# One explicit activation table set at the head of a fused attention and feed-forward kernel

## The chip, the cores and the metric

The kernel runs on one core of one Trainium2 chip. The metric is the device time of one execution in microseconds (us); lower is better. One core has a matrix engine (PE, with its weight loads listed apart as PEld), a vector engine (DVE), a scalar engine that evaluates functions from a loaded table (ACT), a general engine (POOL, which here issues the input DMAs) and SP, which here issues the output DMAs. Each engine works through its own list of instructions in order and waits for the others at semaphores.

## The reference

Eight batches of eight heads attend over 576 tokens plus 16 "beacon" keys that every query may see; the rest is causal. The attention output of all heads, 512 wide, goes through a feed-forward layer with a leaky ReLU.

```python
B, H, S, Nb, D = (8, 8, 576, 16, 64)
k_all = concatenate([beacon_k, k], axis=2)          # 592 keys
scores = scale * matmul(q, k_all.transpose(0, 1, 3, 2))
scores = where(causal, -1e9, scores)
a = exp(scores - scores.max(-1))
a /= a.sum(-1) + 1e-09
attn = matmul(a, v_all)                             # B,H,S,D -> x of 4608 x 512
h = x @ w_in                                        # 512 -> 2048
return maximum(0.01 * h, h) @ w_out                 # 2048 -> 512
```

## The kernel before

**Tiling.** All matmul operands are bf16. The keys of a head lie in five blocks of up to 128 rows, the queries along the free dimension. For one head `stage_scores` makes six score matmuls (L195, 512, 64, 464, 336, 208 and 80 columns, since blocks on the diagonal skip the queries ahead of them) into PSUM tiles `acc`, and ACT turns each into `aT` with an Exp (L202). DVE multiplies the diagonal blocks with a 0/1 mask (L209, L217). No maximum is subtracted. `stage_av` then multiplies `aT` with `v_aug`, whose rows hold 64 values and 64 ones, so that rows 64 to 127 of `av_ps` hold the sum of each query's weights 64 times over (L233, eight matmuls in two halves of 288 queries: 3 and 5). The division is done on ACT as exp(-ln(sum)): a Ln (L243) from PSUM to `lnd`, an Exp with scale -1 (L246) to `recip`; DVE multiplies and writes the head's part of `xT` (L249).

**The feed-forward part.** `moe1_fchunk` makes 128 of the 2048 hidden features for the 576 tokens of a batch: four matmuls of 512 columns and four of 64 (L260), then a Prelu on ACT for each of the two PSUM tiles (L271: `gT` for 512 tokens, `gtail` for 64). `moe2_tchunk` makes 128 tokens of output from 16 matmuls (L282), a copy by DVE (L290) and an output DMA (L291). The 64-token tails of two batches share one further group of 16 matmuls (L296, `moe2_tailpair`).

**Order.** The program is written as 64 steps, one per head. In a step stand: weight loads and loads for the next batch (POOL), the transposes of a pair of heads in even steps (L168 and L174, PE, with DVE copies at L181 and L182), the scores of the head before, the weighted sum of the head before that, and a share of the feed-forward part of the batch before: four chunks of `moe1_fchunk` in steps 1 to 4 of a batch, one `moe2_tchunk` in steps 5, 6, 7 and step 0 of the next. Batch 0 has no feed-forward work, and after the last head the whole feed-forward part of batch 7 stands alone. A tile framework schedules the instructions of each engine from this and sets the waits. The PSUM pools that tie PE to the others are `ps_acc` (4 buffers, shared by scores and both feed-forward layers; released by ACT's Exp or Prelu, or by DVE's copy) and `ps_av` (2 buffers, one per half head; released when L249 has read them). The input tiles `q_nat`, `k_nat` and `v_aug` have two buffers; before each load of `v_aug` DVE writes its ones with a MEMSET (L147).

**Table loads.** No line of the kernel names a table set. The compiler puts an ACT_TABLE_LOAD on ACT's list where the next function needs one, and the profile writes it down under the line of that function: L243 for Ln, L246 for the Exp of the reciprocal, L202 for the Exp of the scores. Prelu (L271) stands behind an Exp and gets none.

Of the kernel before, what the change touches and what calls it, by code (L numbers as in the profile page):

```python
# [15 lines left out]
def kernel(  # L16
# [11 lines left out]
    nc = tc.nc  # L28
# [29 lines left out]
    OTCH = [(i * 128, min(128, S - i * 128)) for i in range((S + 127) // 128)]  # L58

    QCH = [(0, 288), (288, 288)]  # L60

    singles = ctx.enter_context(tc.tile_pool(name="singles", bufs=1))
    inpool = ctx.enter_context(tc.tile_pool(name="inpool", bufs=2))
# [161 lines left out]
    def stage_av(bt, ht, xT, h):  # L225
        v_aug, aT = bt["v_aug"], ht["aT"]
        for (qs, qw) in QCH:
            av = ps_av.tile([128, 512], FP32, name="av_ps", tag="av_ps")
# [213 lines left out]
```

## Time and profile before

| what | value |
|---|---|
| median of 3 runs | 616.53 us (613.58 to 1085.5) |
| span of the profiled execution | 610.7 us |
| PE / ACT / DVE / POOL busy | 470.3 / 512.6 / 174.1 / 120.4 us |
| ACT_TABLE_LOAD on ACT | 161, at 1283 ns each |
| mean granted clock of PE | 0.905 of full |

The page lists no total time of the profiled execution itself; its span, from the first instruction to the last, is 5.8 us under the median and 2.9 us under the lowest run, and these few microseconds lie around it. Busy times are sums of when an engine had something in it, and a busy PE may be one at half its clock, so the durations of single groups of matmuls say more than its share. "Idle before, <- releaser" names the work that ended an engine's wait. Where several instructions of one line stand together, the profile writes the first one's shape and the count.

### The profile page before, as it was taken

What the parts mean: (1) busy time and instruction counts of PE and PEld (TensorE: products, weight loads), DVE (VectorE), ACT (ScalarE), POOL (GpSimd) and SP (SyncE); (2) the same over time, 40 slices, a digit from 0 to 9 for tenths busy, and PEclk for the clock granted to TensorE, in tenths of its full rate; (3) what the DMA queues carried; (4) which work ended last, traced back from release to release, by engine and by line L of the source; (5) the groups of instructions that cost most, each with busy time, mean ns of one, the idle gap of its engine ahead of it and who ended that gap; (6) DMA issues with size and microseconds to landing.
All of it is one profiled execution on the core that took longest, in us unless ns stands there. A gap on an engine that the chain in (4) does not pass through costs nothing.

```text
span 610.7 us, 7832 instructions
## 1 busy us (share of the span) xinstructions
PE 470.3 (77%) x2766; PEld 226.2 (37%) x2816; DVE 174.1 (29%) x557; ACT 512.6 (84%) x1057; POOL 120.4 (20%) x159
## 2 busy tenths in 40 slices
PE   2867677876798697886888777886858876885696
PEld 1323333433344343443444333443424433442342
DVE  4233321342124412234223521234122421132101
ACT  0899989998999969999999979999799978997640
POOL 9885323020230303103230302303000000000000
PEclk9999888996889988997989978899789988897799
DMA  9999638024660706606561526616000100000002
GB/s 93 152 176 170 41 25 55 35 48 27 40 41 34 75 18 41 57 35 58 38 42 36 64 29 39 41 53 57 1 1 18 52 4 15 0 35 18 19 18 69
DMA packets 123432, 28.57 MB, mean 47 GB/s; under 512 B 115712, under 2 KB 117760, under 8 KB 123392
## 3 DMA queue, kind: packets, MB, share of 16 engines
q0 software_dynamic: 118144, 18.62, 41.3%
q1 hardware_dynamic: 5248, 9.44, 4.5%
q8 instruction: 22, 0.36, 0.3%
q14 instruction: 18, 0.15, 0.1%
HBM read 37.22 MB, written 9.44 MB: 76 GB/s over the span
## 4 chain that ended last, share of the span: by engine, by line
ACT 51%; PE 24%; issue 16%; DVE 6%; POOL 1%; DMA 1%; DVEq 0%; POOLq 0%
ACT L243 14%; PE acc L260 11%; ACT aT L202 11%; ACT L246 9%; ACT recip L246 6%; ACT lnd L243 6%; PE acc L195 5%; ACT gT L271 4%; PE acc L282 4%; DVE osb L290 3%; DVE xT L249 3%; PE acc L296 2%; PE av_ps L233 1%; ACT gtail L271 1%; DMA k_nat<-in_k_dram 1%
## 5 line engine op out<-in xcount | busy, mean ns | idle before, releaser
L260 PE MATMUL acc<-xT,w_in_sb 128*128 128x512 bf16 (+1 forms) x996 | 169.9, 329 | 33.0 <-ACT gT L271 25.2
L202 ACT ACTIVATE aT<-acc 128x512 bf16<-128x512 f32 (+5 forms) x384 | 123.6, 408 | 38.7 <-PE acc L195 37.5
L233 PE MATMUL av_ps<-aT,v_aug 128*128 128x288 bf16 (+4 forms) x512 | 85.3, 273 | 59.1 <-DVE xT L249 59.1
L260 PEld LDWEIGHTS <-w_in_sb 128*128 128x128 bf16 x1024 | 82.7, 111 | 118.9 <-issue 77.8
L249 DVE TENSOR_TENSOR xT<-av_ps,recip 64x288 bf16<-64x288 f32 x128 | 53.5, 447 | 253.9 <-ACT recip L246 253.8
L282 PE MATMUL acc<-w_out_sb,gT 128*128 128x512 bf16 x491 | 114.4, 382 | 0.8
L195 PE MATMUL acc<-qT_sb,kT_sb 64*128 64x512 bf16 (+5 forms) x384 | 82.6, 310 | 30.1 <-ACT gT L271 13.9
L243 ACT ACT_TABLE_LOAD x80 | 102.6, 1283 | 1.4
L246 ACT ACT_TABLE_LOAD x79 | 101.4, 1283 | 1.4
L271 ACT ACTIVATE gT<-acc 128x512 bf16<-128x512 f32 x128 | 76.6, 599 | 28.9 <-PE acc L260 26.6
L233 PEld LDWEIGHTS <-v_aug 128*128 128x128 bf16 (+1 forms) x512 | 41.0, 101 | 107.4 <-issue 80.6
L282 PEld LDWEIGHTS <-gT 128*128 128x128 bf16 x512 | 48.8, 98 | 54.7 <-issue 1.6
L124 POOL DMA_DIRECT2D q_nat<-in_q_dram x40 | 33.9, 878 | 98.1 <-PE tp_ps L168 95.1
L246 ACT ACTIVATE recip<-lnd 64x288 f32<-64x288 f32 x128 | 51.4, 436 | 0.9
L217 DVE TENSOR_TENSOR aT<-aT,mask_reg 128x128 bf16<-128x128 bf16 (+1 forms) x256 | 45.9, 212 | 18.8 <-ACT aT L202 16.4
L195 PEld LDWEIGHTS <-kT_sb 64*128 64x128 bf16 (+1 forms) x384 | 28.7, 102 | 59.8 <-issue 48.6
L243 ACT ACTIVATE lnd<-av_ps 64x288 f32<-64x288 f32 x128 | 46.9, 403 | 4.2 <-PE av_ps L233 3.3
L209 DVE TENSOR_TENSOR aT<-aT,mask_reg 128x112 bf16<-128x112 bf16 x64 | 13.5, 211 | 81.3 <-ACT aT L202 80.3
L148 POOL DMA_DIRECT2D v_aug<-in_beacon_v_dram x8 | 4.4, 548 | 156.2 <-PE av_ps L233 156.0
L140 POOL DMA_DIRECT2D k_nat<-in_k_dram x40 | 33.6, 861 | 1.4 <-DMA w_in_sb<-in_moe_w_in_dram 0.7
L157 POOL DMA_DIRECT2D v_aug<-in_v_dram x40 | 33.7, 868 | 0.0
L290 DVE COPY osb<-acc 128x512 f32<-128x512 f32 x32 | 21.9, 684 | 33.4 <-PE acc L282 33.0
(23 smaller groups left out, 185.0 us busy)
## 6 DMA issues: line engine op xcount, KB each, us to landing
out_dram<-osb SPq DMA_DIRECT2D x32, 256.0 KB, 2.0
q_nat<-in_q_dram POOLq DMA_DIRECT2D x32, 128.0 KB, 4.1
k_nat<-in_k_dram POOLq DMA_DIRECT2D x24, 128.0 KB, 4.1
v_aug<-in_v_dram POOLq DMA_DIRECT2D x24, 128.0 KB, 4.2
w_in_sb<-in_moe_w_in_dram POOLq DMA_DIRECT2D x8, 256.0 KB, 7.0
w_out_sb<-in_moe_w_out_dram POOLq DMA_DIRECT2D x8, 256.0 KB, 9.0
out_dram<-osb SPq DMA_DIRECT2D x8, 128.0 KB, 2.3
k_nat<-in_k_dram POOLq DMA_DIRECT2D x8, 112.0 KB, 3.2
```

Of the source, the lines that this page charges most:

```text
L124: nc.gpsimd.dma_start(out=q_nat[0:rows, ci, :, :], in_=q[b, :, s0 : s0 + rows, :].rearrange("h p d -> p h d"),)
L195: nc.tensor.matmul(out=acc[0:rows, 0:cw], lhsT=kT_sb[p0 : p0 + 64, l0_ : l0_ + rows], rhs=qT_sb[p0 : p0 + 64, c0 : c0 + cw], start=True, s ...
L202: nc.scalar.activation(out=aT[0:rows, ci, c0 - off : c0 - off + cw], in_=acc[0:rows, 0:cw], func=AF.Exp, scale=0.125,)
L217: nc.vector.tensor_tensor(out=aT[0:rows, ci, 0:rows], in0=aT[0:rows, ci, 0:rows], in1=mask_reg[0:rows, 0:rows], op=ALU.mult,)
L233: nc.tensor.matmul(out=av[0:128, lo - qs : qw], lhsT=v_aug[0:rows, ci, h, :], rhs=aT[0:rows, ci, lo - off : qs + qw - off], start=(bi == 0 ...
L243: nc.scalar.activation(out=lnd[0:64, 0:qw], in_=av[64:128, 0:qw], func=AF.Ln)
L246: nc.scalar.activation(out=recip[0:64, 0:qw], in_=lnd[0:64, 0:qw], func=AF.Exp, scale=-1.0)
L249: nc.vector.tensor_tensor(out=xT[(h % 2) * 64 : (h % 2) * 64 + 64, h // 2, qs : qs + qw], in0=av[0:D, 0:qw], in1=recip[0:64, 0:qw], op=ALU ...
L260: nc.tensor.matmul(out=acc[:, 0:tw], lhsT=w_in_sb[:, j, fc * 128 : (fc + 1) * 128], rhs=xT[:, j, ts : ts + tw], start=(j == 0), stop=(j == ...
L271: nc.scalar.activation(out=dst, in_=acc[:, 0:tw], func=AF.Prelu, alpha=0.01,)
L282: nc.tensor.matmul(out=acc[0:tw, :], lhsT=gT[:, fc, t0 : t0 + tw], rhs=w_out_sb[:, fc, :], start=(fc == 0), stop=(fc == NF - 1),)
L290: nc.vector.tensor_copy(out=osb[0:tw, :], in_=acc[0:tw, :])
```

## The change

One call is added ahead of the tile pools. It puts one ACT_TABLE_LOAD of the set `natural_log_exp_and_others`, which holds Exp, Ln and Prelu, at the head of ACT's list. No other line is changed; all later lines move down by two, so that L202 is L204, L243 is L245, and so on.

```diff
     QCH = [(0, 288), (288, 288)]
+
+    nc.scalar.preload_act_table_set("natural_log_exp_and_others")

     singles = ctx.enter_context(tc.tile_pool(name="singles", bufs=1))
```

In the built program ACT has 161 ACT_TABLE_LOADs before and 1 after. The same 896 ACTIVATEs are there. The first place is ACT in batch 0, one step before, where `aT<-acc` are the Exps of the scores, `lnd` the Lns and `recip` the Exps of the reciprocal:

```order
L243 ACT_TABLE_LOAD
L243 ACTIVATE lnd<-av_ps 64x288 x2
L246 ACT_TABLE_LOAD
L246 ACTIVATE recip<-lnd 64x288 x2
L202 ACTIVATE aT<-acc 128x512
L202 ACTIVATE aT<-acc 128x64
L202 ACTIVATE aT<-acc 128x464
```

And the same step with the change:

```order
L245 ACTIVATE lnd<-av_ps 64x288 x2
L248 ACTIVATE recip<-lnd 64x288 x2
L204 ACTIVATE aT<-acc 128x512
L204 ACTIVATE aT<-acc 128x64
L204 ACTIVATE aT<-acc 128x464
```

The two loads are gone and the ACTIVATEs stand as they stood. The second place is ACT where the first feed-forward chunks of a batch stand among the Lns, before:

```order
L246 ACT_TABLE_LOAD
L246 ACTIVATE recip<-lnd 64x288 x2
L271 ACTIVATE gT<-acc 128x512
L271 ACTIVATE gtail<-acc 128x64
L271 ACTIVATE gT<-acc 128x512
L271 ACTIVATE gtail<-acc 128x64
L243 ACT_TABLE_LOAD
L243 ACTIVATE lnd<-av_ps 64x288
L246 ACT_TABLE_LOAD
L246 ACTIVATE recip<-lnd 64x288
```

And with the change:

```order
L245 ACTIVATE lnd<-av_ps 64x288
L248 ACTIVATE recip<-lnd 64x288
L273 ACTIVATE gT<-acc 128x512
L273 ACTIVATE gtail<-acc 128x64
L273 ACTIVATE gT<-acc 128x512
L273 ACTIVATE gtail<-acc 128x64
L245 ACTIVATE lnd<-av_ps 64x288
L248 ACTIVATE recip<-lnd 64x288
```

Here too only the loads have gone. The tile framework orders a few matmuls of the first heads of batch 0 otherwise (114 of PE's 5634 rows move). The third place is PE right after the transposes of the queries of the third pair of heads, before:

```order
L168 MATMUL tp_ps<-ident,q_nat 128x64
L174 LDWEIGHTS k_nat
L174 MATMUL tp_ps<-ident,k_nat 128x128
L174 LDWEIGHTS k_nat
L174 MATMUL tp_ps<-ident,k_nat 128x128
```

And with the change:

```order
L170 MATMUL tp_ps<-ident,q_nat 128x64
L197 LDWEIGHTS kT_sb
L197 MATMUL acc<-qT_sb,kT_sb 128x208
L197 LDWEIGHTS kT_sb
L197 MATMUL acc<-qT_sb,kT_sb 80x80
L176 LDWEIGHTS k_nat
```

The last two scores of the first head now stand ahead of the transposes of the third pair's keys instead of behind them. After the first seven heads PE's list is the same; POOL's and SP's are the same throughout, and on DVE one of two multiplications of the first head (L249) moves by one place.

## The prediction

> **What bounds the kernel now.** I read the page's busy times first, then the groups of instructions for the loads, the waits, and then the time line of single steps, since the share of busy time mixes stages.
>
> ```profile
> PE 470.3 (77%) x2766; PEld 226.2 (37%) x2816; DVE 174.1 (29%) x557; ACT 512.6 (84%) x1057; POOL 120.4 (20%) x159
> ACT 51%; PE 24%; issue 16%; DVE 6%; POOL 1%; DMA 1%; DVEq 0%; POOLq 0%
> L243 ACT ACT_TABLE_LOAD x80 | 102.6, 1283 | 1.4
> L246 ACT ACT_TABLE_LOAD x79 | 101.4, 1283 | 1.4
> DVE xT L249 <- ACT recip L246: 253.8, 79, 4.4
> PE av_ps L233 <- DVE xT L249: 59.1, 48, 2.7
> PE acc L260 <- ACT gT L271: 25.2, 16, 2.5
> ```
>
> ACT is the busiest and carries half of the chain that ended last. Two groups of 159 loads (161 are in the program) take 204.0 us of its 512.6. PE's longest waits are for what lies behind loads: the normalised `xT` that frees `av_ps`, and the Prelu that frees `acc`. One step of batch 0 on ACT shows the loads without cover:
>
> ```profile
> 44.11 1.84 ACT L202 ACTIVATE aT<-acc 128x512 bf16<-128x512 f32 x6
> 45.97 1.28 ACT L243 ACT_TABLE_LOAD   x1
> 47.26 0.70 ACT L243 ACTIVATE lnd<-av_ps 64x288 f32<-64x288 f32 x2
> 47.99 1.28 ACT L246 ACT_TABLE_LOAD   x1
> 49.28 0.78 ACT L246 ACTIVATE recip<-lnd 64x288 f32<-64x288 f32 x2
> 50.08 1.84 ACT L202 ACTIVATE aT<-acc 128x512 bf16<-128x512 f32 x6
> ```
>
> The step is 50.08 - 44.11 = 5.97 us, ACT never rests, and 2.6 us are loads. Each load begins 0.02 to 0.03 us after the ACTIVATE before it and the next ACTIVATE follows at once, so a load costs 1.28 us and little else. The Trainium skill (ScalarE: Activation LUTs, What ACT_TABLE_LOAD costs) adds a drain of about 1.38 us to each switch, 2.66 us in all; by it the 159 would be 423 us. These rows have no room for that drain, so they decide.
>
> It would be wrong to take 204 us off the span: that holds only where ACT sets the pace afterwards too. So I cut the span into five pieces and ask in each what PE needs.
>
> ```profile
> 0.00:22.09 22.09, 11.00 (x51) 4.31 (x51) 7.94 (x15) 5.36 (x14) 20.55 (x32) 1.00 1.46 107
> 22.09:63.88 41.79, 28.71 (x137) 12.80 (x137) 14.83 (x58) 41.21 (x85) 26.85 (x36) 1.00 1.65 160
> 63.88:102.81 38.93, 28.09 (x165) 13.58 (x168) 10.05 (x31) 35.77 (x73) 12.98 (x17) 0.82 0.57 37
> 102.81:530.46 427.65, 340.53 (x2071) 166.41 (x2110) 127.01 (x415) 383.70 (x794) 59.99 (x75) 0.90 0.35 37
> 530.46:610.70 80.24, 61.99 (x346) 29.10 (x352) 14.27 (x40) 46.57 (x97) 0.00 (x0) 0.91 0.09 30
> ```
>
> The columns are the length, then busy us (and instructions) of PE, PEld, DVE, ACT, POOL, then PE's clock, DMA share and GB/s. The pieces are the start to the first Ln, seven heads of batch 0, the first part of batch 1, six whole batches (71.3 us each), and the end.
>
> **Start, 22.1 us: unchanged.** The first load lies under the wait for the inputs (ACT is busy 5.36 of 22.09 us), and so will the new one. The reordered rows of PE lie at the end of this piece: half a dozen transposes of about 0.1 us, either way, taken as 0.
>
> **Seven heads of batch 0, 41.8 to 25.9 us.** Without the loads ACT needs 1.84 + 0.70 + 0.78 and the gaps, 3.35 us per head; that is the lower end. PE is busy 28.71 / 7 = 4.1 us per head here, against 2.15 for the same work further on (below), so it runs at about half speed although the clock column says 1.00. If it stays so slow, PE is the bound at 4.1; but then it works without gaps, and the dense stretches of the later trace ran at full clock. I take the middle, 3.7, and 7 x 3.7 = 25.9; the ends give 23.5 and 28.7. The loads of POOL stay ahead:
>
> ```profile
> 34.94 1.72 POOL L98 DMA_DIRECT2D w_in_sb<-in_moe_w_in_dram  x3
> DMA to landing us min/median/max: 5.5/7.0/8.2
> ```
>
> The last part of `w_in_sb` is issued by 36.66 and lands within 8.2, before 45; the first layer would need it at 22.1 + 25.9 + 1.7 = 49.7.
>
> **A whole batch, 71.3 to 51.5 us (53.3 with the tail group).** PE's price of each part is read where it ran without waits at full clock:
>
> ```profile
> 316.85 0.41 PE L195 MATMUL acc<-qT_sb,kT_sb 64*128 64x512 bf16 x2
> 318.91 3.62 PE L282 MATMUL acc<-w_out_sb,gT 128*128 128x512 bf16 x15
> 363.81 4.08 PE L260 MATMUL acc<-xT,w_in_sb 128*128 128x512 bf16 x31
> 370.06 2.12 PE L260 MATMUL acc<-xT,w_in_sb 128*128 128x512 bf16 x15
> ```
>
> (A matmul or two are missing from some rows; each group has 16 or 32.) The second layer is 4 x 3.6 = 14.4. The first layer has 128 matmuls, 3 x 2.12, 2 x 4.13 (one matmul added to 4.08) and a part of 1.95 at the join of two batches (12 and 4 matmuls beside others), 16.6. Between 316.85 and 318.91 stand a head's six scores, seven of eight weighted-sum matmuls and four transposes, 2.06; with the rest 2.15, and eight heads are 17.2. That is 48.2 us of work. ACT has, per batch, 8 x 3.35 and 16 pairs of Prelus at 0.6 (`gT` at 352.97, the next at 353.57, below), 36.4 us, so it is no longer the bound; PE is.
>
> ```profile
> 352.97 0.60 ACT L271 ACTIVATE gT<-acc 128x512 bf16<-128x512 f32 x1
> 353.57 0.60 ACT L271 ACTIVATE gT<-acc 128x512 bf16<-128x512 f32 x1
> 344.59 0.42 PE L233 MATMUL av_ps<-aT,v_aug 128*128 128x288 bf16 x3
> 345.61 2.19 DVE L147 MEMSET v_aug<- 128x2560 bf16 x1 [1.10 <-PE av_ps L233]
> 347.72 0.40 DVE L217 TENSOR_TENSOR aT<-aT,mask_reg 128x128 bf16<-128x128 bf16 x3
> 349.17 0.81 DVE L249 TENSOR_TENSOR xT<-av_ps,recip 64x288 bf16<-64x288 f32 x2 [1.05 <-ACT recip L246]
> 349.77 0.38 PE L233 MATMUL av_ps<-aT,v_aug 128*128 128x288 bf16 x3 [2.56 <-DVE xT L249]
> 375.05 3.78 PE L260 MATMUL acc<-xT,w_in_sb 128*128 128x512 bf16 x16
> ```
>
> What is left of the waits I walked through for one batch by hand. After a second-layer chunk ACT has 3.62 us for 6 Exps' rest, two Lns and two reciprocals, about 2 us: no wait is left there. At the join of two batches one is, and it changes its cause: DVE's MEMSET of 2.19 us stands ahead of the masks and of `xT`. It starts 0.6 us after the last weighted sum of the old batch (345.01) and holds DVE for 2.5 us with the masks (to 348.12); the first half of `xT` needs about 0.45 more and some start-up, so it ends 3.7 us after that sum. PE has 12 first-layer matmuls (1.6 us) and ten transposes (about 0.75) for that time, 2.35 us, and waits about 1.35 (2.56 before). The Lns and Prelus behind it cost PE, by my estimate from the walk, 0.8 us for the buffers of the next two chunks, the scores behind those 0.85, and smaller waits 0.3: 3.3 us per batch. Sum 48.2 + 3.3 = 51.5. Every second batch has the tail group, 3.6 more; six batches are 6 x 51.5 + 3 x 3.6 = 319.8 (427.65 before).
>
> **First part of batch 1, 38.9 to 27.8 us.** It holds 112 first-layer matmuls, 14.5 us, about three and a half heads, 7.3, and the join, 3.0: 24.8. PE comes into it at half clock, and I add 3.0: the first 16 matmuls took 3.78 instead of 2.12 us after such a wait before (375.05, the row above), and some heads' work stands beside them.
>
> The rows for the end, and for the clock further down:
>
> ```profile
> 571.42 1.12 PE L260 MATMUL acc<-xT,w_in_sb 128*128 128x512 bf16 x4 [4.37 <-DVE xT L249]
> 588.22 13.98 PE L282 MATMUL acc<-w_out_sb,gT 128*128 128x512 bf16 x63
> 602.03 3.62 PE L296 MATMUL acc<-w_out_sb,gtail 128*128 128x512 bf16 x15
> 348.00:350.00 2.00, 0.23 (x3) 0.24 (x4) 0.93 (x4) 1.97 (x4) 2.00 (x3) 1.00 1.60 102
> 352.00:354.00 2.00, 0.38 (x1) 0.10 (x1) 0.45 (x1) 1.96 (x5) 0.00 (x0) 0.50 0.37 23
> ```
>
> **The end, 80.2 to 65.4 us.** By the same prices: 2.1 of the first layer, 4 chunks of 3.6, four rests of heads 2.1 + 1.8 + 1.8 + 2.2 and 0.6 for the last sums, 128 matmuls of the first layer 17.0, a wait of 0.7 for the last `xT` (4.37 before, with four loads in its chain), 64 of the second 14.0, the tail 3.6, and from its end to the end of the span 5.05 as before (602.03 + 3.62 to 610.7).
>
> **The sum.** 22.1 + 25.9 + 27.8 + 319.8 + 65.4 = 461.0 us of span. With the 5.8 us by which the median of the runs, 616.53, is above the profiled span of 610.7, that is 467 us.
>
> **Rivals.** *The clock falls at each join.* Around a wait of 2.56 us PE's clock was halved: 1.00 at 348 to 350, 0.50 at 352 to 354, and 16 matmuls took 3.78 us at 375. I leave about 2 us of waits within some 5 us at the join. Before, the six batches ran at a mean clock of 0.90, which is 42.8 us lost, 7.1 per batch, at two places; if the join keeps its half, 3.5 us in each of seven batches, that is 24.5 us: 491. The Trainium skill (TensorE: Matmul & The Clock Gate, Why this matters for your kernels) wants no idle gap over about 3 us for the clock to stay; by it this rival would not happen and the sum stays 467, but the rows show the clock lost after a gap of 2.56 us, so the chance is not nil: 0.15.
>
> *PE runs through.* If the join's waits are covered (the scheduler's other work fills them), batch 0 goes at ACT's 3.35 and batch 1 begins at full clock, 7 x 3.3 + 2.4 + 3.0 = 28.5 us fall away: 438. Against it: DVE's MEMSET stays where it is. 0.12.
>
> ```profile
> PE acc L195 <- DVE osb L290: 9.6, 26, 0.8
> L202 ACT ACTIVATE aT<-acc 128x512 bf16<-128x512 f32 x64 | 38.5, 602 | 24.9 <-PE acc L195 24.1
> L271 ACT ACTIVATE gT<-acc 128x512 bf16<-128x512 f32 x128 | 76.6, 599 | 28.9 <-PE acc L260 26.6 <-remote 1.5
> ```
>
> *More small waits than I count.* Every step leaves PE, ACT and DVE in a ring through 4 and 2 PSUM buffers; if each of 56 heads loses a further 0.7 us (PE lost up to 0.8 to the output copy before, first row), 39 us: 506. 0.10.
>
> *Slower functions, the other side.* If each ACTIVATE were slower from the combined set, ACT would be the bound again: it has 36.4 us per batch against PE's 51.5, so from 1.4 times the duration on it decides, and at 71.3 / 36.4 = 1.96 times nothing would be won; above 2 times it is slower than 616. At 2.1 times, a batch is 76.4 us, 5 us above before, and the time about 660. Against it: a 128x512 Exp and a 128x512 Prelu, different functions, take 602 and 599 ns. 0.02, half of it slower.
>
> That the loads come back elsewhere can be excluded: the built program holds one.
>
> **How the numbers follow.** The forecast has 0.61, and its own range is 452 to 482 (seven heads of batch 0 from 23.5 to 28.7, waits per batch from 1.5 to 5). With the clock rival inside and half of the other two, the range is 445 to 500. A measurement of this kernel tells about 2% from no change. All cases but slower functions are over 2% faster, 0.98; within 2% 0.01, slower 0.01.
>
> **What would show it.** One ACT_TABLE_LOAD; ACT busy near 306 us; heads of batch 0 every 3.4 to 4.0 us; second-layer chunks every 5.4 us within a batch; batches every 51.5 and 55.1 us; PE the first in the chain with over 60%, its clock at 0.95 or more after batch 1; a wait of PE on `xT` of about 1.4 us left at each join, behind the MEMSET. I am wrong if Exps, Lns or Prelus become longer, if PE's clock still falls in each batch, or if PE waits for ACT in the second-layer steps.

## The result and the profile after

| | kernel before | kernel after |
|---|---|---|
| median, us | 616.19 (4 runs, 613.58 to 1085.5) | 454.88 (4 runs, 454.70 to 455.02) |
| ratio | | 0.739, 95% interval 0.7355 to 0.7434 |
| span of the profiled execution, us | 610.7 | 453.0 |
| mean granted clock of PE | 0.905 | 0.998 |

The forecast was 467 us, 445 to 500. One run of the kernel before took 1085.5 us; the ratio leaves it out. The table loads fell from 161 to one, 160 x 1.283 = 205 us of ACT's work, and the time by 161 us, so 0.79 us per us of load. The measured time lies inside the forecast's range, 12 us under its middle.

From the page of the kernel after: the busy times, PE's clock in 40 slices, and the engines in the chain that ended last.

```profile
PE 421.1 (93%) x2816; PEld 207.4 (46%) x2816; DVE 179.3 (40%) x557; ACT 299.5 (66%) x897; POOL 120.4 (27%) x159
...
PEclk9999999999999999999999999999999999999999
...
PE 72%; ACT 14%; DVE 5%; issue 3%; DMA 3%; POOL 2%; POOLq 0%
```

ACT was first in the chain with 51% and has 14% now; PE carries 72% and is busy 93% of a span in which the clock column no longer falls (for batch 0 the column is wrong, as shown below). The waits of the kernel after (what waited, for what, us in total, times, the longest):

```profile
ACT aT L204 <- PE acc L197: 86.2, 36, 13.5
...
PE av_ps L235 <- DVE xT L251: 7.9, 6, 1.5
...
PE acc L262 <- ACT gT L273: 2.9, 7, 0.6
```

The direction has turned round: ACT now waits 86 us for scores, and PE, which waited 59.1 us for `xT` and 25.2 for Prelus, waits 7.9 and 2.9. The span cut at the same places of the program as in the forecast (length, then busy us of PE, PEld, DVE, ACT, POOL, clock, DMA share, GB/s):

```profile
0.00:21.62 21.62, 10.66 (x50) 4.16 (x51) 7.94 (x15) 5.37 (x13) 20.38 (x32) 1.00 1.45 104
21.62:49.91 28.29, 27.82 (x137) 12.85 (x136) 14.54 (x58) 23.63 (x70) 20.89 (x29) 1.00 1.67 176
49.91:75.10 25.19, 22.61 (x170) 11.78 (x169) 10.05 (x31) 20.26 (x60) 16.62 (x22) 1.00 1.66 122
75.10:388.60 313.50, 302.30 (x2115) 151.07 (x2111) 132.09 (x415) 222.36 (x672) 62.48 (x78) 1.00 0.49 51
388.60:453.00 64.40, 57.71 (x356) 27.58 (x352) 14.66 (x40) 27.87 (x82) 0.00 (x0) 0.99 0.11 38
```

| piece | forecast | measured | difference |
|---|---|---|---|
| start | 22.1 | 21.6 | -0.5 |
| seven heads of batch 0 | 25.9 | 28.3 | +2.4 |
| first part of batch 1 | 27.8 | 25.2 | -2.6 |
| six batches | 319.8 | 313.5 | -6.3 |
| end | 65.4 | 64.4 | -1.0 |
| around the span | 5.8 | 1.9 | -3.9 |

The last row is 454.88 - 453.0. The differences sum to -11.9, from 466.8 before rounding to 454.9.

ACT in two steps beside the second layer (time line of the kernel after: start, length, what; in brackets the rest ahead of it and what ended it):

```profile
239.22 1.85 ACT L204 ACTIVATE aT<-acc 128x512 bf16<-128x512 f32 x6 [2.19 <-PE acc L197]
241.10 0.70 ACT L245 ACTIVATE lnd<-av_ps 64x288 f32<-64x288 f32 x2
241.70 0.77 ACT L248 ACTIVATE recip<-lnd 64x288 f32<-64x288 f32 x2
244.53 1.85 ACT L204 ACTIVATE aT<-acc 128x512 bf16<-128x512 f32 x6 [2.06 <-PE acc L197]
```

A step is 244.53 - 239.22 = 5.31 us and ACT rests about 2.1 of them, always for a score of PE. The Lns follow the Exps without a load. PE in the same steps has no wait at all (the two groups left out have none either):

```profile
240.55 3.62 PE L284 MATMUL acc<-w_out_sb,gT 128*128 128x512 bf16 x16
244.10 0.61 PE L197 MATMUL acc<-qT_sb,kT_sb 64*128 64x512 bf16 x3
244.65 0.64 PE L235 MATMUL av_ps<-aT,v_aug 128*128 128x288 bf16 x5
...
245.85 3.62 PE L284 MATMUL acc<-w_out_sb,gT 128*128 128x512 bf16 x16
```

Most of what is left of PE's waits stands at the joins of two batches. DVE at one join:

```profile
257.93 2.19 DVE L149 MEMSET v_aug<- 128x2560 bf16 x1 [0.67 <-PE av_ps L235]
260.04 0.40 DVE L219 TENSOR_TENSOR aT<-aT,mask_reg 128x128 bf16<-128x128 bf16 x3
260.46 0.82 DVE L251 TENSOR_TENSOR xT<-av_ps,recip 64x288 bf16<-64x288 f32 x2
```

And PE at the same join:

```profile
261.06 0.38 PE L235 MATMUL av_ps<-aT,v_aug 128*128 128x288 bf16 x3 [1.54 <-DVE xT L251]
...
263.04 2.12 PE L262 MATMUL acc<-xT,w_in_sb 128*128 128x512 bf16 x16 [0.39 <-ACT gT L273]
```

The reciprocals were done at 258.31 + 0.77 = 259.08 (not shown), so `xT` waits there for DVE, which is in its MEMSET and the masks until 260.44; PE loses 1.54 us, and 0.39 more behind a Prelu.

### The profile page after: what moved, and what is told of

It reads as the page before. It is cut to its first block, busy times and chain, and to the rows that moved or that the text cites. A ratio compares the mean times of both kernels' runs of the same rounds, so it can differ in the third digit from the quotient of the medians.

```text
span 453.0 us, 7721 instructions
## 1 busy us (share of the span) xinstructions
PE 421.1 (93%) x2816; PEld 207.4 (46%) x2816; DVE 179.3 (40%) x557; ACT 299.5 (66%) x897; POOL 120.4 (27%) x159
## 4 chain that ended last, share of the span: by engine, by line
PE 72%; ACT 14%; DVE 5%; issue 3%; DMA 3%; POOL 2%; POOLq 0%
PE acc L284 24%; PE acc L262 16%; PE acc L197 13%; PE av_ps L235 12%; ACT gT L273 4%; ACT recip L248 3%; PE acc L298 3%; ACT lnd L245 3%; ACT aT L204 2%; DVE v_aug L149 2%; DMA q_nat<-in_q_dram 2%; PE tp_ps L176 2%; DVE xT L251 2%; PE tp_ps L170 2%; ACT gtail L273 1%
## 5 line engine op out<-in xcount | busy, mean ns | idle before, releaser
L204 ACT ACTIVATE aT<-acc 128x512 bf16<-128x512 f32 (+5 forms) x384 | 120.0, 411 | 86.6 <-PE acc L197 86.2
L262 PE MATMUL acc<-xT,w_in_sb 128*128 128x512 bf16 (+1 forms) x1024 | 134.8, 287 | 3.4 <-ACT gT L273 2.9
L262 PEld LDWEIGHTS <-w_in_sb 128*128 128x128 bf16 x1024 | 70.3, 98 | 65.4 <-issue 5.5
L235 PE MATMUL av_ps<-aT,v_aug 128*128 128x288 bf16 (+4 forms) x512 | 81.0, 270 | 9.5 <-DVE xT L251 7.9
L197 PE MATMUL acc<-qT_sb,kT_sb 64*128 64x512 bf16 (+5 forms) x384 | 79.7, 302 | 3.0 <-ACT aT L204 0.7
L284 PEld LDWEIGHTS <-gT 128*128 128x128 bf16 x512 | 48.5, 98 | 53.8
L245 ACT ACTIVATE lnd<-av_ps 64x288 f32<-64x288 f32 x128 | 47.7, 403 | 24.6 <-PE av_ps L235 22.9
L235 PEld LDWEIGHTS <-v_aug 128*128 128x128 bf16 (+1 forms) x512 | 37.8, 102 | 44.3 <-issue 29.8
L219 DVE TENSOR_TENSOR aT<-aT,mask_reg 128x128 bf16<-128x128 bf16 (+1 forms) x256 | 46.4, 212 | 20.6 <-ACT aT L204 15.7
L292 DVE COPY osb<-acc 128x512 f32<-128x512 f32 x32 | 22.1, 691 | 64.8 <-PE acc L284 64.8
L197 PEld LDWEIGHTS <-kT_sb 64*128 64x128 bf16 (+1 forms) x384 | 26.7, 101 | 40.7 <-issue 27.3
L170 PE MATMUL tp_ps<-ident,q_nat 128*128 128x128 bf16 (+1 forms) x160 | 21.6, 231 | 8.7 <-DMA q_nat<-in_q_dram 8.5
L273 ACT ACTIVATE gtail<-acc 128x64 bf16<-128x64 f32 x128 | 28.6, 223 | 0.0
```

The source lines that it names most:

```text
L197: nc.tensor.matmul(out=acc[0:rows, 0:cw], lhsT=kT_sb[p0 : p0 + 64, l0_ : l0_ + rows], rhs=qT_sb[p0 : p0 + 64, c0 : c0 + cw], start=True, s ...
L204: nc.scalar.activation(out=aT[0:rows, ci, c0 - off : c0 - off + cw], in_=acc[0:rows, 0:cw], func=AF.Exp, scale=0.125,)
L219: nc.vector.tensor_tensor(out=aT[0:rows, ci, 0:rows], in0=aT[0:rows, ci, 0:rows], in1=mask_reg[0:rows, 0:rows], op=ALU.mult,)
L235: nc.tensor.matmul(out=av[0:128, lo - qs : qw], lhsT=v_aug[0:rows, ci, h, :], rhs=aT[0:rows, ci, lo - off : qs + qw - off], start=(bi == 0 ...
L245: nc.scalar.activation(out=lnd[0:64, 0:qw], in_=av[64:128, 0:qw], func=AF.Ln)
L262: nc.tensor.matmul(out=acc[:, 0:tw], lhsT=w_in_sb[:, j, fc * 128 : (fc + 1) * 128], rhs=xT[:, j, ts : ts + tw], start=(j == 0), stop=(j == ...
```

## The experiments

All kernels but one (it says so) are the kernel after with one edit, or with two that were tried apart. In the runs that follow the kernel before took 610.97 to 612.61 us on the same chips, and single runs of it spread over 1 to 2%, those of the changed kernels over up to 0.8%; so I compare the changed kernels by their own times with 454.88, and take a difference for real where the trace shows its place. That this can be done across the chips is seen in `half_loads`: up to its edit it keeps within 0.2 us of the kernel after (the last second-layer chunk ahead of it starts at 200.73 and 200.94).

**delay_m2: is ACT off the path beside the second layer?** In the 28 heads of batches 1 to 7 that stand beside a second-layer chunk, the Ln of the first half is repeated three times more: 84 instructions of about 0.4 us, 33 us of ACT that nothing needs.

```diff
-            nc.scalar.activation(
-                out=lnd[0:64, 0:qw], in_=av[64:128, 0:qw], func=AF.Ln
-            )
+            for _ in range(4 if extra and qs == 0 else 1):
+                nc.scalar.activation(
+                    out=lnd[0:64, 0:qw], in_=av[64:128, 0:qw], func=AF.Ln
+                )
...
+                     extra=b >= 1 and h in (0, 5, 6, 7))
```

> 28 heads (those that stand beside a second-layer chunk, batches 1 to 7) repeat the Ln of their first half three times more, about 1.2 us of ACT each, 33 us in all, behind the same waits and with the same result. In the profile of the change ACT rests 2.06 us in each of these steps. Theory (PE sets the pace, ACT has slack there): 455 us, 452 to 460. Rival (ACT still sets the pace, every microsecond on it counts): 455 + 33 = 488.

Measured 456.8 us (456.5 to 457.35). ACT in the same two steps:

```profile
241.26 1.85 ACT L204 ACTIVATE aT<-acc 128x512 bf16<-128x512 f32 x6 [0.87 <-PE acc L197]
...
246.56 1.85 ACT L204 ACTIVATE aT<-acc 128x512 bf16<-128x512 f32 x6 [0.74 <-PE acc L197]
```

The step is still 5.30 us and only the rest shrinks, from 2.1 to 0.8. 33 us of ACT cost 1.9, and that not beside the second layer: the first second-layer chunk starts 2.2 us later than in the kernel after (81.35 against 79.15) and the last group at the end 2.0 (432.52 against 430.49), so the loss lies at the entry into batch 1, where one of the 28 places stands and PE's clock is 0.50 from 58 to 60 in place of 1.00. ACT's work beside the second layer, which the forecast costs at nothing, is covered by PE.

**delay_m2b: where does the cover end?** The same with 7 in the place of 4, 66 us in all, 2.4 per step.

> The same 28 heads repeat that Ln six times more, about 2.35 us of ACT each, 66 us in all, nearly what the two loads per head took. Theory: that is 0.3 us over the slack of 2.06, so each step goes from 5.3 to 5.6 or a little more, 463 to 472 us. Rival (all of it counts): 521. Rival (ACT's time does not matter at all): 455.

Measured 472.19 us (471.35 to 472.58), 17.3 more than without. ACT has no rest left:

```profile
243.33 1.86 ACT L204 ACTIVATE aT<-acc 128x512 bf16<-128x512 f32 x6
245.21 3.20 ACT L246 ACTIVATE lnd<-av_ps 64x288 f32<-64x288 f32 x8
248.45 0.78 ACT L249 ACTIVATE recip<-lnd 64x288 f32<-64x288 f32 x2
249.25 1.84 ACT L204 ACTIVATE aT<-acc 128x512 bf16<-128x512 f32 x6
```

This step is 249.25 - 243.33 = 5.92 us, 0.62 above 5.30. That 28 x 0.62 = 17.4 comes near the 17.3 is chance. A whole batch is 1.8 to 2.0 us longer, some 0.46 for each of its four steps, and 4.0 us are lost ahead of the first of them (83.19 against 79.15), behind a wait at the entry into batch 1:

```profile
56.59 0.59 PE L235 MATMUL av_ps<-aT,v_aug 128*128 128x288 bf16 x3 [3.33 <-DVE xT L252]
```

The forecast had 0.3 us a step or a little more and no loss at the entry; the result is 0.2 us above its range. Beside the second layer ACT becomes the bound once about 2 us are added to a step. The two loads that stood in each such step were 2 x 1.28 = 2.57 us, beyond that cover.

**half_loads: do the loads explain the whole difference?** One Sqrt of 64 x 8 elements behind the first Ln of batch 4, whose result nothing reads. Sqrt is not in the preloaded set, so from there on the compiler again places a load at each turn between Ln and Exp.

```diff
+            if extra and qs == 0:
+                junk = singles.tile([64, 8], FP32, name="junk")
+                nc.scalar.activation(
+                    out=junk[0:64, 0:8], in_=lnd[0:64, 0:8], func=AF.Sqrt
+                )
...
+                     extra=s - 2 == 4 * H)
```

> The changed kernel with one small extra ACTIVATE (a square root of 64x8 into a tile that nobody reads) behind the first Ln of batch 4. It forces another table, and from there on the compiler places real loads as in the kernel before; up to there the program has the one load. Theory (the gain is made step by step wherever loads are gone): 210 us as in the changed kernel up to that place, then 325 as before, 2 around the span: 537, 525 to 550, with PE's clock at 0.99 in the first part and 0.90 in the second. Rival (the gain comes from the start, from the order of batch 0 or from a clock that stays up once it is up): 455 to 470.

Measured 541.13 us (539.62 to 544.12). The page's two groups of loads (busy us and mean ns), then the span cut where they begin (columns as above):

```profile
L253 ACT ACT_TABLE_LOAD x41 | 52.6, 1283 | 0.7
L245 ACT ACT_TABLE_LOAD x41 | 52.6, 1283 | 0.7
```

```profile
0.00:210.00 210.00, 189.20 (x1219) 93.02 (x1240) 91.81 (x283) 141.55 (x423) 91.82 (x124) 1.00 1.02 87
210.00:538.30 328.30, 257.51 (x1548) 125.29 (x1577) 84.51 (x275) 270.30 (x559) 28.52 (x36) 0.90 0.27 32
```

With two single ones more, 84 loads came back, 107.8 us, and cost 541.13 - 454.88 = 86.3: 0.80 us per us. The 76 that stay away, 97.5 us, then account for the other 75.0 of the gain, 0.77 per us. PE's clock is 1.00 before the place and 0.90 behind it, inside one execution. So the gain follows the loads in both parts alike, and the lost clock of the kernel before followed from them. A load takes 1.28 us and the next ACTIVATE starts 0.01 us behind it (one that begins at 332.35 is followed by a Ln at 333.64). The Trainium skill (ScalarE: Activation LUTs, What ACT_TABLE_LOAD costs) has a drain of about 1.38 us beside it at each switch; no row here shows one.

The rate of 0.8 is a mean over unlike parts: the six batches gained 114.2 us for 120 loads, 0.74 per us, and the first part of batch 1 gained 13.7 for 12, 0.89. Inside a batch it differs more. One batch of the kernel before, cut at PE's second-layer chunks: three steps beside the second layer, then the rest (one more such step, the join and the first layer).

```profile
318.91:338.81 19.90, 17.10 (x97) 8.23 (x97) 7.82 (x27) 18.39 (x39) 0.00 (x0) 1.00 0.10 35
338.81:390.51 51.70, 40.73 (x262) 20.12 (x265) 14.09 (x43) 45.53 (x97) 13.64 (x17) 0.87 0.59 48
```

And the same batch of the kernel after:

```profile
235.25:251.86 16.61, 16.61 (x99) 7.79 (x97) 8.26 (x26) 9.73 (x32) 0.00 (x0) 1.00 0.33 61
251.86:289.52 37.66, 35.47 (x267) 18.13 (x265) 14.52 (x44) 27.39 (x83) 13.64 (x17) 1.00 0.72 57
```

The three steps lost six loads, 7.7 us, and gained 3.3, 0.43 per us, since PE's own 5.30 us stand close behind ACT's. The rest lost 14 loads, 18.0 us, and gained 14.0, 0.78 per us, and only there had the clock fallen. So most of the gain was made where `delay_m2` and the next two runs change nothing; what bounds the steps beside the first layer is known from PE's rows (busy 35.47 of 37.66 us after) and from `half_loads`, not from an experiment of its own.

**short_m2_after and short_m2_before: is it PE that bounds the one, and ACT the other?** In each of the 32 second-layer chunks the last 4 of 16 matmuls are left out, in the kernel after and in the kernel before.

```diff
-        for fc in range(NF):
+        for fc in range(NF - 4):
...
-                stop=(fc == NF - 1),
+                stop=(fc == NF - 5),
```

> The changed kernel with 4 of the 16 matmuls left out in each of the 32 second-layer chunks (the last quarter of the hidden features is not added; the tail group is whole). Theory (PE sets the pace): 32 x 4 x 0.2165 = 27.7 us less, 427, 424 to 432. Rival (ACT or the ring through the PSUM buffers sets it): 445 to 455.

> The kernel before with the same 4 of 16 matmuls left out in each second-layer chunk. Theory (ACT with its loads sets the pace in the steps; only the last chunks at the end stand alone on PE): 3.5 us less from the end and next to nothing from the 28 steps, 609 to 616. Rival (PE sets the pace there too): 616 - 27.7 = 588.

After: 427.25 us (427.16 to 427.52), 27.6 less. ACT, still resting:

```profile
227.94 1.85 ACT L204 ACTIVATE aT<-acc 128x512 bf16<-128x512 f32 x6 [1.33 <-PE acc L197]
...
232.37 1.85 ACT L204 ACTIVATE aT<-acc 128x512 bf16<-128x512 f32 x6 [1.19 <-PE acc L197]
```

The step is 232.37 - 227.94 = 4.43 us, 0.87 less than with all 16 matmuls, and 32 x 0.87 = 27.8. All of the work taken from PE came off the time.

Before: 616.46 us against 610.97 for the kernel before, ratio 1.009 (1.0037 to 1.0142). The same edit that saves 27.6 us in one kernel saves nothing in the other. I had expected 3.5 us less; it came out 5.5 longer, just above my 609 to 616. The wait of PE that grew, in the profiled run (608.14 us, the lowest of them):

```profile
PE av_ps L233 <- DVE xT L249: 71.1, 40, 2.7
```

Work taken from PE came back as waiting (71.1 us against 59.1), and the mean clock is 0.87 to 0.88 in the runs behind this figure, where the kernel before has 0.90 to 0.92. I take the small loss for that, but did not test it.

**no_memset: does the wait at the join come from the MEMSET?** Two fixed `v_aug` tiles are used in turn. Their ones are written once, ahead of the first head, and loads touch only the values.

```diff
-        v_aug = inpool.tile([128, NKB, H, D + 64], BF16, name="v_aug")
+        v_aug = v_bufs[len(batch_tiles) and (max(batch_tiles) + 1) % 2]
...
-        nc.vector.memset(v_aug[:, :, :, D : D + 64], 1.0)
...
+    for vname in ("v_aug_a", "v_aug_b"):
+        vb = singles.tile([128, NKB, H, D + 64], BF16, name=vname)
+        nc.vector.memset(vb[:, :, :, D : D + 64], 1.0)
+        v_bufs.append(vb)
```

> The changed kernel with two fixed tiles for v_aug whose ones are written once at the start, so that no MEMSET stands on DVE at a join of two batches. Theory: at six joins PE's waits of 1.54 and 0.39 us go, 11.6 us: 443, 441 to 447. Rival (the waits are put down to the wrong cause, and the Ln, reciprocal and multiplication behind them end as late): 452 to 455.

Measured 442.09 us (441.01 to 442.76), 12.8 less. Of the seven joins six have a MEMSET. At five of them a batch is 2.2 to 2.4 us shorter (PE's first second-layer chunks 52.0 us apart in place of 54.3, or 48.5 in place of 50.9), against 1.54 + 0.39 forecast; at the entry into batch 1, where PE waits for queries, 0.5 us is gained, and at the last join, without a MEMSET, 0.2. PE at a join:

```profile
203.03 0.43 PE L175 MATMUL tp_ps<-ident,k_nat 128*128 128x128 bf16 x5
203.30 0.38 PE L234 MATMUL av_ps<-aT,v_aug_a 128*128 128x288 bf16 x3
```

The weighted sum follows the transposes without a wait. The MEMSET was the cause, as forecast. It was there before the change too, but `xT` waited for ACT's reciprocal even after it (the row at 349.17 in the prediction); taking it out of the kernel before was not tried.

**warm: what holds PE at half clock in batch 0?** After the change the seven heads of batch 0 are the piece that came out longer than forecast. PE works there without gaps at half speed: four score matmuls take 1.32 us at 26.54 and at 42.51 in the kernel after, against 0.75 for the same four at full clock. In this run 27 idle matmuls of 512 columns stand among the first transposes, where PE waits for inputs.

```diff
+    def warm_up(nat, ci, rows):
+        for _ in range(3):
+            wps = ps_acc.tile([128, 512], FP32, name="acc", tag="acc")
+            nc.tensor.matmul(
+                out=wps[:, :],
+                lhsT=nat[0:rows, ci, 0:2, :],
+                rhs=nat[0:rows, ci, 0:8, :],
...
+            if first:
+                warm_up(q_nat, ci, rows)
```

> The changed kernel with 27 idle matmuls of 512 columns (results not read) among the first transposes, where PE waits for the inputs anyway, so that PE comes to the first scores after steady work. Theory (batch 0 goes at PE's half clock, 4.0 us a head, and the clock stays up once raised): batch 0 at 3.4 us a head, 4 to 5 us less, and about 1 more from the first head: 447 to 451. Rival (with less to do than ACT, PE falls back to half clock, or the half clock is not the cause): 453 to 457.

Measured 452.47 us (451.93 to 453.34), between the two. The first scores, the wait of 0.94 at 26, and the stretches around it:

```profile
16.48 0.75 PE L212 MATMUL acc<-qT_sb,kT_sb 64*128 64x512 bf16 x4 [0.43 <-DVE kT_sb L199]
...
26.34 0.59 PE L250 MATMUL av_ps<-aT,v_aug 128*128 128x288 bf16 x3 [0.94 <-DVE xT L266]
```

```profile
25.00:30.00 5.00, 4.06 (x21) 1.59 (x17) 3.19 (x11) 4.93 (x16) 3.98 (x5) 0.58 2.09 168
30.00:35.00 5.00, 5.00 (x26) 2.48 (x26) 2.03 (x8) 4.29 (x14) 4.80 (x8) 0.50 1.99 158
35.00:40.00 5.00, 4.93 (x27) 2.44 (x28) 2.55 (x11) 3.58 (x12) 4.83 (x8) 0.50 1.96 156
40.00:45.00 5.00, 4.94 (x23) 2.19 (x22) 2.71 (x11) 4.68 (x16) 2.46 (x4) 0.50 1.10 185
45.00:50.00 5.00, 5.00 (x29) 2.57 (x28) 1.69 (x5) 3.80 (x12) 3.48 (x5) 0.53 1.25 207
```

The clock was full at first and fell near 26, where PE waited for `xT`; then it stayed at 0.50 until nearly 50, when the first layer had begun, although PE was busy almost all the time. Whether the wait let it fall, or the work ahead of it, is not shown. The Trainium skill (TensorE: Matmul & The Clock Gate, What's actually happening) has the full clock come after about 3.4 us of sustained work; these rows have nearly 20 us of sustained work at half (30 to 50). So being busy is not enough, and a new theory was wanted: the scores contract over 64 rows where other matmuls use 128, and batch 0 has no feed-forward matmuls beside them.

**tall and tall_warm: is it the height of the scores?** In batch 0 alone the scores contract over all 128 rows of a transposed pair. That adds the products of two heads, so batch 0 isn't the reference's. `tall_warm` has the idle matmuls too.

```diff
-        p0 = par * 64
+        p0, pe = (0, 128) if tall else (par * 64, par * 64 + 64)
...
-                    lhsT=kT_sb[p0 : p0 + 64, l0_ : l0_ + rows],
-                    rhs=qT_sb[p0 : p0 + 64, c0 : c0 + cw],
+                    lhsT=kT_sb[p0:pe, l0_ : l0_ + rows],
+                    rhs=qT_sb[p0:pe, c0 : c0 + cw],
```

> The scores of batch 0 alone contract over all 128 rows of the transposed pair (two heads' products added, so batch 0 is not the reference's) instead of 64; the durations at one clock should be equal. What holds PE at half its clock in batch 0 is open. If it is the 64-row scores, the clock rises once PE is dense, heads of batch 0 come near ACT's 3.35 us instead of 4.04, and the time falls to 449 to 453 us. If it is something else (short matmuls with gaps, the transposes, the input DMAs), heads stay at 4.0 us and the time is 454 to 456.

> The same 128-row scores in batch 0, and the 27 idle matmuls of the run warm ahead of it, so that the clock is full when the heads begin. If the 64-row scores let the clock fall at 26 us and held it at half until 48, it now stays full or comes back within a few us, heads take about 3.4 us, batch 0 is 3 to 5 us shorter and the time is 447 to 450 us. If the scores' height has no part in it, the clock falls at the same waits and the time is that of the run warm, 452 to 453.

Measured 448.57 us (447.37 to 448.71), a little under the range, and 448.06 (446.76 to 449.67). In `tall`, four slow scores of PE and four like them some us later, with the wait behind them; then a stretch that can be set beside the one of `warm`:

```profile
15.00 1.33 PE L197 MATMUL acc<-qT_sb,kT_sb 128*128 128x512 bf16 x4 [0.50 <-DVE kT_sb L184]
...
23.99 0.75 PE L197 MATMUL acc<-qT_sb,kT_sb 128*128 128x512 bf16 x4
25.77 0.38 PE L235 MATMUL av_ps<-aT,v_aug 128*128 128x288 bf16 x3 [1.03 <-DVE xT L251]
```

```profile
35.00:40.00 5.00, 3.50 (x29) 2.34 (x28) 3.26 (x12) 4.92 (x16) 4.86 (x9) 1.00 1.94 159
```

PE begins at half clock and is at full before 24; nothing but the rows of the scores was changed. It keeps the full clock over a wait of 1.03 us, and in a stretch where it is busy only 3.50 of 5 us; in `warm` the clock was lost around a wait of 0.94 and stayed away at 4.93 of 5. ACT's Exps of two heads, five apart, start at 25.59 and 41.90, so a head now takes (41.90 - 25.59) / 5 = 3.26 us, ACT's own work, the lower end of the forecast. In `tall_warm` the clock fell after a wait of 1.51 us for queries that ended at 27.7, and came back by 35 (the clock is 0.52 from 30 to 35 and 1.00 from 35 to 40). With 64-row scores it did not come back in 20 us.

**Versions that are faster.** `no_memset_warm` joins the two edits of those names. `padded` makes the tall scores of batch 0 right: the queries are copied into two tiles per pair, one for each head, with zeros in the other head's 64 rows. `no_memset_padded` joins this with the fixed `v_aug` tiles.

```diff
+                nc.vector.tensor_copy(
+                    out=pads[par][p0 : p0 + 64, :], in_=qT_ps[p0 : p0 + 64, 0:S])
...
+            nc.vector.memset(qp[z0 : z0 + 64, :], 0.0)
...
+            p0, pe, qT_sb = 0, 128, pt["pads"][par]
```

> Both edits together. If they work in different places they add: 437 to 441 us if both theories hold, 443 if only the MEMSET's does.

> The queries of batch 0 are copied into tiles whose other 64 rows hold zeros, so that its scores contract over 128 rows and the result is the reference's; one more DVE copy (about 0.4 us) per pair of heads. If the height of the scores sets the clock in batch 0, as the run tall showed, the time is that of tall or a little more, 447 to 451 us, against 455. If what counts is that all rows hold data other than zeros, the clock stays at half and the time is 454 to 457.

> The padded scores of batch 0 and the two fixed v_aug tiles together. If the two gains are in different places and add up (12.8 us for the MEMSETs, about 6 for the clock in batch 0), 434 to 439 us. The entry into batch 1 loses its MEMSET too, so a little more than the sum may be gained there; if batch 0 is hidden behind DVE's extra copies, 441 to 443.

Measured 439.15 us (438.29 to 440.85; the two edits had gained 12.8 and 2.4 apart and gain 15.7 together), 449.52 (448.82 to 450.09) and 434.98 (434.32 to 436.07). Padding the queries with zeros does nearly what data do (449.52 against the 448.57 of `tall`), so the rows that a matmul contracts over matter here, and not whether both operands hold data in them. `padded` alone gains 5.4 us and the MEMSETs 12.8, together 19.9, the fastest kernel here: 0.714 of the kernel before (0.7106 to 0.7168). The 1.7 beyond the sum fits the entry into batch 1. PE there in `padded`:

```profile
47.44 0.58 PE L255 MATMUL av_ps<-aT,v_aug 128*128 128x288 bf16 x3 [2.26 <-DVE xT L271]
47.84 1.13 PE L282 MATMUL acc<-xT,w_in_sb 128*128 128x512 bf16 x4
```

And in `no_memset_padded`:

```profile
46.26 0.38 PE L254 MATMUL av_ps<-aT,v_aug_b 128*128 128x288 bf16 x3 [0.41 <-DVE xT L270]
46.62 0.65 PE L281 MATMUL acc<-xT,w_in_sb 128*128 128x512 bf16 x4
```

With the MEMSET there PE waits 2.26 us and comes out of it at half clock (1.13 us for four matmuls that take 0.65); without it the wait is 0.41 and the four take 0.65.

## Why the prediction was right, point by point

- **ACT no longer the bound, PE instead.** Right, and shown from both sides: 33 us more of ACT cost 1.9, 27.7 us less of PE gave 27.6, and leaving out the same matmuls in the kernel before gave nothing. These runs test the steps beside the second layer; beside the first, where most of the gain was made, it rests on PE's busy share.
- **A load costs 1.28 us and little else.** Right by the rows of `half_loads`. ACT is busy 299.5 us; near 306 was forecast.
- **Batch 0, 3.7 us a head.** The middle was wrong, the upper end right: 28.29 / 7 = 4.04. Of the two reasons weighed, "works without gaps" was true and "so full clock" was not. `tall` shows what held the clock at half: the 64-row scores.
- **Entry into batch 1, 3.0 us for the half clock.** Too much, by about 2 us. The first 12 matmuls of the first layer took 2.49 us in the kernel after, against 1.63 at a later join, and the next ones ran at full clock. With the 128-row matmuls of the first layer the clock came back within these 12, so 2.49 - 1.63 = 0.9 us is lost there. The wait at this join, 1.45 us, is for queries from the input DMA and not for the MEMSET that the forecast had. That this piece and batch 0 together come out right, 53.5 us against 53.7, is luck: a term too low and one too high.
- **A batch, 51.5 and 55.1 us.** 50.9 and 54.3 (235.25 and 289.52 are the first second-layer chunks of two batches); 313.5 / 6 = 52.25 on average, where the forecast has 53.3. The work was a little low and the waits too high: PE is busy 302.3 us in the six batches, the forecast's work is 6 x 48.2 + 3 x 3.6 = 300.0; it is idle 11.2 us, 1.9 a batch, where I had 3.3. At the join shown 1.54 stands for the forecast's 1.35 behind the MEMSET and 0.39 for its 0.8; the 0.85 for the scores and the 0.3 of small waits were not there, and five of the seven joins have the wait behind the MEMSET, not all.
- **Second-layer chunks every 5.4 us.** 5.30.
- **The end, 65.4.** 64.4. **Around the span, 5.8.** 1.9: I carried over the distance between a profiled run and a median of a kernel whose runs spread by 1 to 2%, which was not a constant; a run's time is 2 us above its own span here (455.02 and 453.0), and in a later run of the kernel before too (612.61 and 610.7). This is a third of the whole miss and has nothing to do with the change.
- **Rivals.** The clock does not fall at the joins: it is 1.00 over the six batches, with waits of 1.54 us in them. The margin is small, though: in `padded` it fell at one later join too, where behind a wait of 1.88 us for `xT` (at 255.28) four matmuls of the first layer took 1.04 us in place of 0.65. PE does not run through either, because of the MEMSET and the half clock of batch 0; `no_memset_padded` is without both, and 435 us is near the 438 that this rival gave. There are not more small waits. The functions are not slower from the combined set: a 128x512 Prelu takes 598 ns, 599 before.

## What to carry to other kernels

Before costing a removed load (or any work on the engine that seems to bound), look in each stage for what the next engine needs per step: beside the second layer a load gave 0.43 of its time, since PE's own 5.30 us per step stood close behind ACT's, and in the rest of the batch shown 0.78, where PE's clock came back too. Then look for what was hidden behind the old bound, a MEMSET of 2.19 us in this case, which was worth 12.8 us once the loads were gone. And where matmuls of half height are much of PE's work, read the clock from durations: padding them to 128 rows cost one small copy per pair of heads and gave 5.4 us.

## What was not expected of the hardware

- PE stayed at half its clock for nearly 20 us while it was busy 99% of the time (`warm`, 30 to 45 us at 0.50), with 64-row scores in the mix. `tall` differs from the kernel after in the rows of batch 0's scores alone; it reached the full clock within 9 us of the first score and kept it over a wait of 1.03 us, where the kernel after is still at half at 42.51. The transposes, the weighted sums and the input transfers are the same program in both. In later batches the 64-row scores stand beside feed-forward matmuls and the clock stays full; how large a share of them is needed was not tried.
- The clock column is 1.00 for batch 0 of the kernel after, where the matmuls take 1.32 us in place of 0.75. In `warm`, where the clock changes within the stretch, the column says 0.50 for the same durations. So a column of 1.00 at the start of a trace is no evidence of a full clock.
